# Another order of all pieces of a fused chunk attention and gated convolution, with other homes for the tiles

## The chip, the core and the metric

The kernel runs on one core of a Trainium2 chip. The metric is the time of one execution on the device, in microseconds, as the median of several runs. The core has five engines, each with its own queue that is worked off in order: TensorE (PE, matmuls; PEld is its weight load), VectorE (DVE), ScalarE (ACT), GpSimd (POOL) and SyncE (SP), which here issues every DMA. They wait for one another by semaphores alone.

## The reference

Eight batches, eight heads, 576 positions, 64 numbers a head. Attention is over chunks of 64 positions that don't see each other; its result x, put side by side over the heads (512 channels), goes through a gated convolution.

```python
scores = (1/8) * matmul(q_chunk, k_chunk.T)             # 64 x 64 for each batch, head and chunk
attn = exp(scores - scores.max(-1))
attn = attn / (attn.sum(-1) + 1e-09)
x = matmul(attn, v_chunk)                               # to (batch, 576, 512)
gate = sigmoid(sum over 5 taps of conv_w[k] * x shifted by 4 - k positions, within a batch)
out = ((gate * (x @ w_val)) @ w_out)
```

## The kernel before, in words

The 4608 positions of all batches are cut into 9 groups (g = 0 to 8) of 512. A group is worked in *pieces*: small functions, each of which issues one or a few instructions. The string `ORDER` (line 18 on) lists all 1,131 pieces with their arguments, and the loop at the end of the kernel calls them in that order. Every instruction is issued through one helper (`run`, line 158), which keeps this order on each engine, so all rows of the profile name line 158, and the order of the list is the order of every queue. The table `SLOTS` says which buffer each tile gets, in the order of their creation: `ld` (inputs, 6), `ps` (one PSUM bank each, 4), `big` (two banks each, 2), `acc` (4), `t2` (512 wide, 29, shown as t, t2a to t2r and so on), `t4` (1024 wide, 12). A new tile in a buffer waits until all readers of the old one are through.

The pieces, with g, then the pair p (four of the eight heads, 0 or 1; pair 0 0 is worked in two halves) or the block of 128 channels (0 to 3):

- Loads: `lq`, `lk`, `lv` (q, k, v of a pair, 512 KB), `lw` (128 rows of a weight matrix), `lc` (the taps' table).
- Attention: `S` scores (PE; two of them a pair, 16 instructions each), `mx` their maxima over 64 (DVE). Then one of two ways. Either `sb` subtracts the maxima (DVE), `ex` takes the exponential (ACT), `sm` sums it and takes the reciprocal (DVE, two instructions). Or `ng` scales the maxima (DVE, tiny), `ea` takes exponential and sum in 16 small steps on ACT (32 instructions in the trace), and `rc` finishes the reciprocal (DVE, two tiny ones). `nm` multiplies by the reciprocal (1024 wide). `T` transposes on PE (8 instructions), `ec` copies the result, `A` multiplies by v (PE, 32 instructions).
- x: `xc` copies it from PSUM, `xr` copies it rounded to fp32r, and the remainder x - rounded(x) comes either from `xd` (one subtraction on DVE) or from `xn` and `xe` (PE subtracts with two matmuls against minus the identity, ACT copies).
- Convolution: `k0` the first tap, `k` each of the four others (DVE, a SCALAR_TENSOR_TENSOR on `acc`), `sg` the tanh of it (ACT).
- Value product: `V` (three matmuls of 512 columns: weights and x in high and low part), `F` the same in fp32 for the first group; `vc` copies the result out, `gs` multiplies it with the gate (`gm`: both in one).
- Output product: `gr` rounds, `gd` takes the remainder, `P` three matmuls, `oc` evicts, `st` stores.
- Weights are split into high and low parts in nine small steps (`w1` to `w9`, `wb`); `hl` sets the halo of x; `W` is a number of matmuls without use.

A letter at a name's end puts the piece on another engine: `D` on DVE, `G` on POOL. Without it `nm`, `gd`, `wb` are on POOL, `k0`, `oc`, `xc`, `vc` on ACT, `w1`, `w3`, `w7`, `gs` on DVE. So `gd 0 3` is a remainder on GpSimd and `gdD 0 3` the same on VectorE.

```python
def nm(g, p, *half):
...
    run(on.tensor_tensor, out=out, in0=e, in1=r, op=ALU.mult)
...
def gd(g, m, on=G):
    gl[g, m] = tile_of("gl", [P, T], F32R)
    run(on.tensor_tensor, out=gl[g, m], in0=gt[g, m], in1=gh[g, m].bitcast(F32), op=ALU.subtract)
```

Of the kernel before, what the change touches and what calls it, by code (L numbers as in the profile page):

```python
# [22 lines left out]
F 0 1 0,nm 0 1,lw o 3,F 0 2 0,k0 0 0,w6 v 0,xc 0 0 1,w2 v 3,sb 1 0,w2 v 1,w1G o 0,F 0 3 0,T 0 1,w4 v 3,S 1 1 0,w6 v 2,
lq 2 0,ec 0 1,S 1 1 1,ex 1 0,wb v 2,w4 v 1,wb v 0,A 0 1,lw o 2,lk 2 1,w7 v 3,w5 o 0,W 8,F 0 0 0,w7G v 1,lv 1 0,k0 0 1,
xr 0 1,F 0 2 1,mx 1 1,sm 1 0,w3G o 0,lq 2 1,sb 1 1,k 0 0 4,w1 o 3,S 2 0 0,xc 0 1 0,w2 o 0,nm 1 0,k 0 0 2,ex 1 1,
sm 1 1,xc 0 1 1,w6 v 3,S 2 0 1,xn 0 1,xe 0 1,F 0 3 1,V 0 2 2,hl 1,mx 2 0,T 1 0,sb 2 0,w6 v 1,w3 o 3,w5 o 3,w4 o 0,
F 0 1 1,nm 1 1,k 0 0 1,lq 3 0,S 2 1 0,S 2 1 1,lk 3 0,ec 1 0,lw o 1,ex 2 0,k0 0 3,A 1 0,lv 3 0,F 0 0 1,w5 o 2,mx 2 1,
w7G o 0,xc 1 0 1,wb v 3,sm 2 0,w5 o 1,sb 2 1,w1G o 2,V 0 3 2,lv 1 1,V 0 1 2,k 0 0 3,V 0 0 2,k0G 0 2,w1G o 1,xr 1 0,
w3G o 1,V 0 2 3,w6 o 0,k 0 1 1,T 1 1,xd 1 0,w2 o 2,nm 2 0,xc 1 0 0,ex 2 1,lq 4 0,V 0 0 3,V 0 3 3,ec 1 1,w2 o 3,vc 0 3,
S 3 0 0,wbD v 1,A 1 1,S 3 0 1,k 0 2 4,vc 0 2,k0 1 0,V 1 1 0,V 1 2 0,xr 1 1,sm 2 1,V 1 2 1,mx 3 0,lk 3 1,xd 1 1,  # L30
V 1 1 1,xc 1 1 0,lq 3 1,lv 3 1,ng 3 0,k 0 2 1,V 0 1 3,V 1 2 2,xc 1 1 1,sg 0 0,T 2 0,w3 o 2,lv 2 0,k 0 1 2,V 1 1 2,
gm 0 0,V 1 3 0,k 0 1 4,k 0 3 2,k 0 2 3,nm 2 1,w4 o 3,ea 3 0,k 0 3 1,V 1 2 3,k 0 1 3,k0 1 3,V 1 3 1,V 1 1 3,T 2 1,
# [10 lines left out]
oc 0 0,k0G 2 2,k 2 0 3,P 0 1 3,P 0 3 3,nm 4 0,lq 5 0,oc 0 1,P 0 2 3,k0 2 3,sg 1 1,T 4 0,k 2 1 2,k 2 0 4,V 3 3 0,
xc 3 1 0,k 2 2 2,oc 0 2,V 3 1 0,lk 5 0,rc 4 1,V 3 0 0,gs 1 2,lk 5 1,k 2 3 2,V 3 1 1,ec 4 0,sg 1 3,gs 1 1,S 5 0 0,
sg 2 0,S 5 1 0,k0 3 3,k 2 1 1,S 5 0 1,oc 0 3,S 5 1 1,gs 1 3,mx 5 1,gr 1 0,gd 1 0,nm 4 1,V 3 1 2,gr 1 2,V 3 1 3,
k 2 1 3,V 3 3 1,V 3 2 0,lq 6 0,mx 5 0,V 3 0 1,lk 8 0,k0 3 0,gr 1 1,k 2 2 3,sb 5 0,vc 3 1,sg 2 1,V 3 3 2,ng 5 1,
gdD 1 2,V 3 3 3,lv 4 1,gr 1 3,k 2 2 4,k0 3 2,k 2 3 1,V 3 2 1,gd 1 1,V 3 0 2,lk 6 0,vc 3 3,k 2 3 3,P 1 0 0,ea 5 1,
P 1 1 0,P 1 1 1,k 2 2 1,k 3 2 4,k 3 3 1,lq 6 1,gdD 1 3,P 1 1 2,k 2 3 4,V 3 2 2,k 3 0 2,T 4 1,V 3 0 3,k 3 2 3,k 3 0 1,
V 3 2 3,ec 4 1,P 1 1 3,S 6 0 0,S 6 0 1,A 4 0,lk 6 1,vc 3 2,oc 1 1,sg 2 3,P 1 3 0,gs 2 0,xr 4 0,k 3 0 3,rc 5 1,mx 6 0,
P 1 3 1,P 1 2 0,vc 3 0,P 1 0 1,lv 5 1,xc 4 0 0,xd 4 0,sg 2 2,gs 2 1,ex 5 0,xc 4 0 1,gs 2 3,P 1 2 1,k0 3 1,P 1 0 2,  # L50
P 1 3 2,gr 2 1,V 4 2 0,P 1 2 2,P 1 3 3,lq 7 1,oc 1 3,S 6 1 0,S 6 1 1,gr 2 0,nm 5 1,hl 4,sb 6 0,A 4 1,gd 2 1,k 3 0 4,
gs 2 2,P 1 2 3,V 4 2 1,gr 2 3,k 3 1 2,xr 4 1,P 1 0 3,sm 5 0,sg 3 0,k 3 2 2,gd 2 0,lv 5 0,k0 4 0,nm 5 0,P 2 3 0,xd 4 1,
# [5 lines left out]
xc 5 0 1,gr 3 0,nm 6 0,T 6 0,k 4 2 3,ec 6 0,xd 5 1,k0 5 2,nmD 6 1,k0 5 1,P 2 0 3,oc 2 0,k 4 3 3,V 5 1 1,S 7 0 0,
gd 3 2,S 7 1 0,S 7 1 1,gr 3 1,k0 5 3,S 7 0 1,lk 8 1,k 5 2 2,vc 4 1,lv 6 1,V 4 0 1,k 4 2 2,V 4 0 2,gs 3 3,V 5 0 0,
gr 3 3,k0 5 0,k 4 0 2,mx 7 1,V 4 0 3,V 5 0 1,gd 3 0,st 0 1,mx 7 0,lv 8 1,st 2 1,k 4 0 3,sb 7 1,gdD 3 1,k 4 1 1,gd 3 3,  # L60
V 5 0 2,k 4 2 1,V 5 1 2,vc 4 0,ng 7 0,k 5 2 3,P 3 1 0,k 5 0 3,k 4 0 1,P 3 0 0,P 3 1 1,V 5 1 3,k 4 1 3,V 5 0 3,P 3 1 2,
T 6 1,P 3 0 1,ex 7 1,P 3 1 3,k 4 3 4,k 4 1 2,P 3 0 2,k 4 3 1,k 5 0 4,vc 5 1,ea 7 0,P 3 3 0,lq 8 0,oc 3 1,P 3 3 1,
# [596 lines left out]
```

## Time and profile before

| what | value |
|---|---|
| median of 3 runs | 283.56 us (281.74 to 283.76) |
| profiled execution | 281.89 us, span 280.1 us |
| PE busy | 258.9 us (92%), 3333 matmuls |
| DVE busy | 239.3 us (85%), 330 instructions |
| ACT busy | 195.2 us (70%), 499 instructions |
| POOL busy | 113.1 us (40%), 92 instructions |
| moved by DMA | 42.47 MB, mean 152 GB/s |
| PE's granted clock, mean | 0.994 |

Busy time is what an engine spends in instructions; two that overlap count once. A row of the timeline gives start, length and tiles; neighbours on DVE overlap by some 0.1 us, so the cost of one in a run is the distance of two starts. A wait is put down to the engine whose semaphore came last. Tile names stand without buffer numbers: `big<-ld,ld` are scores, `ps<-t,v_hi` is a value product, `ps<-o_hi,t` an output product, `acc<-x,cw,acc` a tap.

### The profile page before, as it was taken

To read this page: it belongs to the slowest core of one execution; us is meant where nothing else is said; L and a number is where in the kernel's file an instruction comes from. 1 tells how busy PE (TensorE), PEld (TensorE's weight loads), DVE (VectorE), ACT (ScalarE), POOL (GpSimd) and SP (SyncE) were. 2 spreads that over 40 slices of the span, in tenths; PEclk is the share of its full clock that TensorE was granted. 3 is DMA by queue.
4 is the path that set the end of the run, shared out by engine and by line. 5 is a ranking of instruction groups with operands and counts; after the bars stand their busy time and mean duration, and the time that the engine had idled before them with its cause. 6 is when DMAs were issued, how large, how long until landed. Compare 5 with 4: busy or idle time off the path is not lost.

```text
span 280.1 us, 7958 instructions
## 1 busy us (share of the span) xinstructions
PE 258.9 (92%) x3333; PEld 216.6 (77%) x3333; DVE 239.3 (85%) x330; ACT 195.2 (70%) x499; POOL 113.1 (40%) x92
## 2 busy tenths in 40 slices
...
GB/s 230 414 412 411 400 280 53 216 92 288 77 64 239 3 94 210 150 136 170 75 118 0 307 145 192 0 120 220 6 37 0 111 5 152 0 171 16 115 187 150
DMA packets 14291, 42.47 MB, mean 152 GB/s; under 512 B 1712, under 2 KB 1712, under 8 KB 14256
## 3 DMA queue, kind: packets, MB, share of 16 engines
...
HBM read 32.53 MB, written 9.44 MB: 150 GB/s over the span
## 4 chain that ended last, share of the span: by engine, by line
DVE 53%; PE 21%; ACT 14%; DMA 5%; issue 5%; SPq 0%; DVEq 0%; ACTq 0%
DVE acc L158 22%; PE ps L158 19%; DVE t L158 9%; DVE mx L158 5%; DVE rs L158 5%; ACT t L158 5%; DVE e_row L158 4%; ACT e_row L158 4%; DMA acc<-in_moe_w_val 4%; ACT x L158 2%; PE big L158 2%; DMA ld<-in_q 2%; DVE t2q L158 1%; DVE x L158 1%; DVE t4a L158 1%
## 5 line engine op out<-in xcount | busy, mean ns | idle before, releaser
L158 DVE SCALAR_TENSOR_TENSOR acc<-x,cw,acc 128x516 f32<-128x516 f32 (+1 forms) x144 | 111.7, 817 | 3.2 <-ACT acc L158 2.9
L158 PE MATMUL ps<-t,v_hi 128*128 128x512 f32 x240 | 85.1, 395 | 2.9 <-ACT t2f L158 2.1
L158 PEld LDWEIGHTS ps<-t,v_hi 128*128 128x128 f32 x240 | 45.5, 190 | 11.5 <-ACT t2f L158 2.5
L158 PE MATMUL ps<-t,v_lo 128*128 128x512 f32 x120 | 45.9, 383 | 0.0
L158 POOL TENSOR_TENSOR t<-e_row,rs 128x1024 f32<-128x1024 f32 (+1 forms) x12 | 23.2, 1936 | 30.0 <-DVE rs L158 30.0
L158 PEld LDWEIGHTS big<-ld,ld 64*64 64x64 f32 x1152 | 19.5, 139 | 15.0 <-issue 9.7
L158 ACT ACTIVATE e_row<-big,mx 128x64 f32<-128x64 f32 x96 | 28.6, 357 | 2.5 <-DVE mx L158 2.5
L158 PE MATMUL big<-ld,ld 64*64 64x64 f32 x1152 | 22.0, 226 | 8.7 <-DMA ld<-in_q 6.6
L158 PE MATMUL ps<-o_hi,t 128*128 128x512 f32 x80 | 29.9, 381 | 0.0
L158 ACT COPY x<-big 128x512 f32<-128x512 f32 (+3 forms) x42 | 19.7, 520 | 12.5 <-PE big L158 6.2
L158 DVE TENSOR_REDUCE mx<-big 128x16 f32<-128x1024 f32 (+1 forms) x19 | 21.8, 1151 | 5.1 <-PE big L158 5.1
L158 PEld LDWEIGHTS ps<-t,v_lo 128*128 128x128 f32 x120 | 22.8, 190 | 3.3 <-issue 0.5
L158 ACT ACTIVATION_READ_ACCUMULATOR e_row<-big,mx 128x1 f32 x96 | 23.8, 249 | 0.0
L158 PE MATMUL big<-t,ld 64*64 64x64 f32 x1088 | 19.4, 220 | 4.4 <-issue 2.4
L158 PEld LDWEIGHTS big<-t,ld 64*64 64x64 f32 x1088 | 17.6, 135 | 6.7 <-issue 2.1
L158 ACT COPY t<-ps 128x512 f32<-128x512 f32 x27 | 16.7, 625 | 8.4 <-PE ps L158 5.8
L158 ACT ACTIVATE t<-big 128x1024 f32<-128x1024 f32 x15 | 15.8, 1077 | 7.1 <-PE big L158 7.1
L158 ACT ACTIVATE e_row<-e_row 128x1024 f32<-128x1024 f32 (+1 forms) x12 | 12.0, 1001 | 11.4 <-DVE e_row L158 11.4
L158 ACT CAST t<-big 128x1024 fp32r<-128x1024 f32 x17 | 17.3, 1019 | 2.0 <-PE big L158 2.0
L158 ACT ACTIVATE acc<-x,cw 128x516 f32<-128x516 f32 (+1 forms) x24 | 17.8, 756 | 0.0
L158 POOL TENSOR_SCALAR acc<-x,cw 128x516 f32<-128x516 f32 (+1 forms) x9 | 14.9, 1657 | 4.8 <-ACT x L158 4.8
L158 PEld LDWEIGHTS ps<-o_hi,t 128*128 128x128 f32 x80 | 15.1, 189 | 2.2
...
## 6 DMA issues: line engine op xcount, KB each, us to landing
...
```

The lines of the kernel that those rows point to most:

```text
L158: return tc.keep_in_program_order(fn(*args, **kwargs))
```

## The change

All pieces are listed in another order and `SLOTS` gives other buffers; no function changes. By the two lists (1,131 pieces before, 1,134 after) the following changes besides the order:

- `ea` 6 to 7: pairs 5 0, 6 1, 7 1, 8 1 take the place of 4 1, 5 1, 7 0 (3 0, 4 0 and 8 0 stay); `sb`, `sm`, `ex` one less each, `ng` and `rc` one more.
- `xn`/`xe` 2 to 4 (1 0, 1 1, 2 0, 3 1 instead of 0 1, 2 1); `xd` 15 to 13.
- `nm` on DVE 3 to 7 (one of them a half), on POOL 16 to 12. `gd` on DVE 11 to 16, on POOL 25 to 20. `oc` on DVE 8 to 11, on ACT 28 to 25. `xc` on DVE 4 to 5 pieces.
- `k0` on ACT 24 to 19, on POOL 9 to 13, on DVE 3 to 4.
- `wb` on DVE 4 to 1, on POOL 4 to 7; `w1` on DVE 4 to 2, on POOL 5 to 7; `w3` on DVE 4 to 6, on POOL 5 to 3. `gm` 2 to 1, `vc` and `gs` one more each.

```diff
-ORDER = """zi,lk 0 0,zw,zr 1,lc,lq 0 0,lw v 2,lk 0 1,w1 c 0,S 0 0 1,w3G c 0,lq 0 1,lw v 0,mx 0 0 1,sb 0 0 1,S 0 0 0,lw v 3,
+ORDER = """lk 0 0,lq 0 0,zr 1,S 0 0 0,mx 0 0 0,lq 0 1,lc,sb 0 0 0,zw,lk 0 1,S 0 0 1,w3 c 0,w1 c 0,lw v 2,mx 0 0 1,lw v 0,
...
 SLOTS = dict(
-    ld="012345012350412305241203123142135013450420534024035425",
+    ld="012345012340512304152403240104120354251041045342502402",
...
```

**The first DMAs, on SP.** Before; `ld` tiles are q, k and v, `acc` tiles are raw weights, `raw_cw` is the taps' table:

```order
L158 DMA ld_75<-in_k 128x1024
L158 DMA raw_cw<-in_moe_conv_w 128x40
L158 DMA ld_81<-in_q 128x1024
L158 DMA acc_83<-in_moe_w_val 128x1024
L158 DMA ld_85<-in_k 128x1024
L158 DMA ld_108<-in_q 128x1024
L158 DMA acc_110<-in_moe_w_val 128x1024
L158 DMA acc_132<-in_moe_w_val 128x1024
L158 DMA ld_134<-in_k 128x1024
```

After:

```order
L159 DMA ld_71<-in_k 128x1024
L159 DMA ld_73<-in_q 128x1024
L159 DMA ld_95<-in_q 128x1024
L159 DMA raw_cw<-in_moe_conv_w 128x40
L159 DMA ld_101<-in_k 128x1024
L159 DMA acc_124<-in_moe_w_val 128x1024
L159 DMA acc_127<-in_moe_w_val 128x1024
L159 DMA acc_147<-in_moe_w_val 128x1024
L159 DMA ld_176<-in_v 128x1024
```

The taps' table went from second to fourth, q from third to second; the second half's q and k stand ahead of all weights, and three parts of `w_val` follow before k of the next pair.

**DVE, about pair 8 1.** Before, from the reciprocal of its sums (`rs_2680`) to its normalisation (`t4a<-e_row_65,rs_2680`):

```order
L158 RECIPROCAL rs_2680<-rs_2680 128x16
L158 SCALAR_TENSOR_TENSOR t2s<-t_2630,t2d 128x512
L158 SCALAR_TENSOR_TENSOR acc_2265<-x_2129,cw,acc_2265 128x516 x2
L158 SCALAR_TENSOR_TENSOR acc_2269<-x_2129,cw,acc_2269 128x516
L158 TENSOR_SCALAR t_2703<-big_2661 128x1024
L158 SCALAR_TENSOR_TENSOR t_2708<-t2i,t2m 128x512
L158 SCALAR_TENSOR_TENSOR t2q<-t2e,t_2050 128x512
L158 SCALAR_TENSOR_TENSOR t2g<-t2a,t_2354 128x512
L158 TENSOR_SCALAR acc_2794<-x_2621,cw 128x516
L158 SCALAR_TENSOR_TENSOR acc_2794<-x_2621,cw,acc_2794 128x516
L158 TENSOR_REDUCE mx_2816<-big_2715 128x16
L158 TENSOR_TENSOR t4a<-e_row_65,rs_2680 128x1024
```

After, from the reciprocal of its sums (`rs_2816`, summed by ScalarE) to its normalisation (`t_3065`):

```order
L159 TENSOR_SCALAR rs_2816<-rs_2816 128x16
L159 RECIPROCAL rs_2816<-rs_2816 128x16
L159 TENSOR_REDUCE mx_2954<-big_2917 128x16
L159 TENSOR_TENSOR t_2956<-t2c,t2n 128x512
L159 TENSOR_SCALAR mx_2954<-mx_2954 128x16
L159 SCALAR_TENSOR_TENSOR acc_2765<-x_2594,cw,acc_2765 128x516
L159 TENSOR_SCALAR acc_3018<-x_2861,cw 128x516
L159 SCALAR_TENSOR_TENSOR acc_2761<-x_2594,cw,acc_2761 128x516
L159 SCALAR_TENSOR_TENSOR acc_2765<-x_2594,cw,acc_2765 128x516
L159 TENSOR_TENSOR t2h<-t2m,t_2867 128x512
L159 SCALAR_TENSOR_TENSOR acc_2761<-x_2594,cw,acc_2761 128x516
L159 TENSOR_TENSOR t_3065<-e_row_65,rs_2816 128x1024
```

The reduction that stood ahead of the reciprocal (`TENSOR_REDUCE rs`) is gone, two small instructions are in its place, and two remainders of y (`t_2956<-t2c,t2n` and `t2h<-t2m,t_2867`, both `gdD`) stand between, where before there were products with the gate.

**PE, at the first value products of the last group.** `t_3331` is its rounded x, `t_3357` the remainder that DVE's `xd 8 0` writes. Before:

```order
L158 MATMUL ps_3187<-o_hi,t_3141 128x512
L158 MATMUL ps_3187<-o_lo,t_3141 128x512
L158 MATMUL ps_3187<-o_hi,t_3155 128x512
L158 MATMUL ps_3368<-t_3331,v_hi 128x512
L158 MATMUL ps_3368<-t_3331,v_lo 128x512
L158 MATMUL ps_3368<-t_3357,v_hi 128x512
L158 MATMUL ps_3376<-t_3331,v_hi 128x512
L158 MATMUL ps_3376<-t_3331,v_lo 128x512
L158 MATMUL ps_3376<-t_3357,v_hi 128x512
L158 MATMUL ps_3345<-o_hi,t2m 128x512
L158 MATMUL ps_3345<-o_lo,t2m 128x512
L158 MATMUL ps_3345<-o_hi,t2p 128x512
```

After (`t_3341` and `t_3350`):

```order
L159 MATMUL ps_3355<-o_hi,t_2867 128x512
L159 MATMUL ps_3355<-o_lo,t_2867 128x512
L159 MATMUL ps_3355<-o_hi,t2h 128x512
L159 MATMUL ps_3396<-t_3341,v_hi 128x512
L159 MATMUL ps_3396<-t_3341,v_lo 128x512
L159 MATMUL ps_3396<-t_3350,v_hi 128x512
L159 MATMUL ps_3405<-t_3341,v_hi 128x512
L159 MATMUL ps_3405<-t_3341,v_lo 128x512
L159 MATMUL ps_3405<-t_3350,v_hi 128x512
L159 MATMUL ps_3396<-t_3341,v_hi 128x512
L159 MATMUL ps_3396<-t_3341,v_lo 128x512
L159 MATMUL ps_3396<-t_3350,v_hi 128x512
```

The value products of the last group follow output products in both; after the first of them stand 195 matmuls to the end, where there were 201, and 30 matmuls lie between the place of `xd 8 0` in the list and the first of them, where there were 6.

## Rows read from the trace of the kernel before

**Rows 1.** The page, part 1: busy us of each engine (share), instructions.
```profile
PE 258.9 (92%) x3333; PEld 216.6 (77%) x3333; DVE 239.3 (85%) x330; ACT 195.2 (70%) x499; POOL 113.1 (40%) x92
```

**Rows 2.** Chain of waits, 228 to 280: start us, length us, what.
```profile
231.91 1.22 DVE t L158
...
233.18 43.24 PE ps L158 x199
...
276.44 0.59 ACT t L158
```

**Rows 3.** Waits of DVE: waited for, us in total, times, longest.
```profile
DVE mx L158 <- PE big L158: 5.1, 3, 3.3
DVE t L158 <- ACT x L158: 3.4, 2, 2.0
```

**Rows 4.** Timeline of DVE, 160 to 187: start us, us, instruction, [idle before].
```profile
160.95 10.74 DVE L158 SCALAR_TENSOR_TENSOR acc<-x,cw,acc 128x516 f32<-128x516 f32 x16
...
177.61 1.23 DVE L158 TENSOR_TENSOR t<-big,t 128x1024 fp32r<-128x1024 f32 x1 [1.97 <-ACT x L158]
178.75 1.23 DVE L158 TENSOR_REDUCE rs<-e_row 128x16 f32<-128x1040 f32 x1
...
180.18 0.63 DVE L158 SCALAR_TENSOR_TENSOR t2s<-t,t2d 128x512 f32<-128x512 f32 x1
...
185.18 0.68 DVE L158 SCALAR_TENSOR_TENSOR t2g<-t2a,t 128x512 f32<-128x512 f32 x1
185.78 0.48 DVE L158 TENSOR_SCALAR acc<-x,cw 128x516 f32<-128x516 f32 x1
186.18 0.75 DVE L158 SCALAR_TENSOR_TENSOR acc<-x,cw,acc 128x516 f32<-128x516 f32 x1
```

**Rows 5.** Timeline of PE, 131 to 139.
```profile
131.18 1.91 PE L158 MATMUL big<-ident,t 128*128 128x128 f32 x16
132.85 0.46 PE L158 MATMUL ps<-o_hi,t2r 128*128 128x512 f32 x1
...
136.26 2.10 PE L158 MATMUL big<-t,ld 64*64 64x64 f32 x128
138.29 0.48 PE L158 MATMUL ps<-o_hi,t2q 128*128 128x512 f32 x1
```

**Rows 6.** Timeline, DVE beside POOL, four places.
```profile
21.99 1.08 DVE L158 SCALAR_TENSOR_TENSOR t<-t,t 128x512 uint32<-128x512 uint32 x1
...
40.87 1.58 POOL L158 TENSOR_SCALAR acc<-x,cw 128x512 f32<-128x512 f32 x1
...
41.36 1.41 DVE L158 SCALAR_TENSOR_TENSOR acc<-x,cw,acc 128x512 f32<-128x512 f32 x2
...
147.43 1.34 POOL L158 TENSOR_TENSOR t2s<-t,t2l 128x512 fp32r<-128x512 f32 x1 [3.83 <-ACT t2l L158]
...
147.56 1.77 DVE L158 SCALAR_TENSOR_TENSOR acc<-x,cw,acc 128x516 f32<-128x516 f32 x1
...
255.68 1.18 DVE L158 SCALAR_TENSOR_TENSOR t2c<-t2l,t 128x512 f32<-128x512 f32 x1
```

**Rows 7.** Timeline of SP, the first issues.
```profile
1.15 0.42 SPq L158 DMA_DIRECT2D raw_cw<-in_moe_conv_w  x1
1.62 0.42 SPq L158 DMA_DIRECT2D ld<-in_q  x1
```

**Rows 8.** By stretch: busy us of PE, PEld, DVE, ACT, POOL; PEclk granted; DMA.
```profile
70.00:80.00 10.00, 10.00 (x55) 8.67 (x55) 9.97 (x16) 9.21 (x40) 2.17 (x1) 1.00 0.14 54
140.00:150.00 10.00, 7.93 (x34) 6.50 (x33) 8.83 (x10) 4.86 (x10) 4.75 (x3) 0.85 0.22 83
```

**Rows 9.** Timeline of PE and DVE, 145 to 153.
```profile
145.80 0.48 PE L158 MATMUL ps<-t,v_hi 128*128 128x512 f32 x1 [2.06 <-ACT t2f L158]
...
152.27 1.42 DVE L158 SCALAR_TENSOR_TENSOR acc<-x,cw,acc 128x516 f32<-128x516 f32 x2 [2.93 <-ACT acc L158]
```

**Rows 10.** Chain of waits, 73 to 80.
```profile
73.84 4.85 ACT e_row L158 x32
```

**Rows 11.** Groups by line: busy us, mean ns, idle before.
```profile
L158 PE MATMUL big<-t,minus 128*128 128x512 f32 x4 | 1.4, 423 | 0.0
```

More of the change, by code (lines that the diff above doesn't have):

```diff
@@ L23 @@
[L23 to L32, printed above, removed]
@@ L43 @@
[L43 to L52, printed above, removed]
@@ L58 @@
[L58 to L62, printed above, removed]
@@ new lines @@
+hl 3,oc 0 1,gr 1 2,mx 5 0,V 3 1 1,lq 5 1,k 2 0 4,ng 5 0,k 2 2 4,xc 3 1 1,V 3 0 0,V 3 2 0,xr 3 1,xc 3 1 0,k 2 3 4,
+k 2 2 2,lq 6 0,k 2 1 2,nm 4 0,k0 3 0,lq 7 0,V 3 2 1,lk 5 1,k 2 0 2,k 2 1 4,k 3 0 3,xn 3 1,xe 3 1,ea 5 0,lk 6 0,
+k 2 0 1,V 3 3 0,V 3 3 1,k 2 1 3,V 3 3 2,k 3 0 2,gd 1 1,T 4 0,k 2 1 1,k 2 3 1,ec 4 0,V 3 3 3,k 2 2 1,V 3 2 2,V 3 2 3,
+V 3 0 1,sg 2 0,gd 1 0,k 3 0 4,vc 3 3,gs 2 0,V 3 1 2,S 5 1 0,k 2 2 3,S 5 1 1,k 2 3 3,ex 4 1,gdD 1 2,k 3 0 1,gr 1 3,
+vc 3 2,rc 5 0,A 4 0,sg 2 2,P 1 3 0,gdD 1 3,nm 5 0,V 3 0 2,sm 4 1,V 3 0 3,xc 4 0 1,k0 3 1,V 3 1 3,gr 2 0,mx 5 1,
@@ new lines @@
+k0 6 2,V 6 1 2,k0 6 0,xr 7 0,gs 4 1,k 6 0 4,gs 5 3,V 5 1 2,ea 8 1,V 6 0 2,st 3 0,gs 4 3,V 5 1 3,V 6 2 0,k 6 3 4,
+k 6 2 3,xd 7 0,V 6 2 1,k 6 0 3,vc 5 1,V 6 2 2,gr 4 2,xc 7 0 0,V 6 3 0,gr 5 3,V 6 0 3,T 7 1,k 6 2 1,vc 6 0,gdD 4 0,
+V 6 2 3,V 6 3 1,gr 4 3,k 6 1 4,xcD 7 0 1,gs 5 2,gr 4 1,hl 7,V 6 1 3,V 6 3 2,sg 5 0,V 6 3 3,ec 7 1,S 8 0 0,S 8 0 1,
+gd 4 2,rc 8 1,mx 8 0,gdD 4 1,vc 6 1,ng 8 0,vc 6 3,A 7 1,P 4 3 0,P 4 0 0,vc 6 2,P 4 1 0,P 4 2 0,k 6 0 2,P 4 3 1,
+k0D 7 1,P 4 1 1,sg 5 1,P 4 2 1,k 6 3 1,st 3 3,gd 4 3,st 1 2,k0G 7 0,P 4 1 2,k 6 1 2,ea 8 0,gdD 5 3,k 6 3 3,P 4 0 1,
```

132 lines of the change are left out of this document (74 added, 58 removed).

## The prediction

> **What bounds the kernel now.** I read the page first. TensorE (PE) is busy 258.9 us of 280.1 and VectorE (DVE) 239.3 [rows 1]: both are near full, ScalarE (ACT) and GpSimd (POOL) are not, so which of the two limits a stretch has to be read from who hands over to whom. The chain of waits shows the end: the last remainder of x (`xd 8 0`) ends on DVE at 233.13, and from 233.18 PE works through 43.24 us without a gap, then one eviction and a store, until 280.1 [rows 2]. So the time is DVE's clock at the last remainder, plus PE's work behind it, plus a tail of 3.7 us. Ahead of that, DVE is what PE waits for; it idles itself for 5.1 us on scores (3.3 of them at the start) and 3.4 on ScalarE [rows 3], little beside its work. A TensorE that is 92% busy is the wrong place to look for what an order changes: its work is fixed, and what it loses is what DVE hands over late.
>
> Hence the measure: at a handover, DVE's work ahead of it in the order plus PE's work behind it. Waits come on top in both kernels.
>
> **Unit prices**, by starts in a run of work [rows 4]: a tap (`k`) 10.74 / 16 = 0.67 us; a full-width operation (`mx`, `sb`, `xd`, `nm`) 1.14; `sm` with its reciprocal 1.43; a 512-wide one (`gs`, `gd`, `w4`, `w7`, `wb`, `oc`) 0.60; `k0` 0.40. PE takes 43.24 / 199 = 0.217 a matmul [rows 2], 0.84 for eight transposes (1.67 for two times eight) and 2.03 for the 64 instructions (128 records) of two products [rows 5].
>
> **The price of GpSimd.** A tap that starts 0.13 us behind a `gd` on POOL takes 1.77 us instead of 0.67 [rows 6]: it waits until POOL's instruction is over. POOL's one-input `k0` beside two taps costs them nothing: 1.41 us for both [rows 6]. In the timeline 22 two-input DVE operations stand over 0.2 us above their price, the first at 21.99, the last at 255.68 [rows 6], 16.9 us together; 19 of them, 14.2 us, before 233. POOL has 42 two-input operations there (`nm`, `gd`, `wb`, `w7`), so I charge DVE 0.34 us for each, between 0 and 1.1 by the single rows.
> The Trainium skill, page "SBUF — State Buffer", section "Who interferes with whom", says that a DVE instruction with two SBUF inputs and a GpSimd instruction that reads SBUF exclude each other for a whole instruction. For `gd` the trace agrees (1.77); for the one-input `k0` it does not (1.41 for two); by the page this change, which gives POOL four more `k0`, would be worth less (a rival below).
>
> **The change, part by part.** Counted from the two lists up to `xd 8 0` (DVE):
> - Pair 5 0, 6 1, 7 1, 8 1 instead of 4 1, 5 1, 7 0 on ScalarE sums: one `sb` (1.14) and one `sm` (1.43) less, `ng` and `rc` more (0.4 with all): -2.1.
> - Two remainders to TensorE: two `xd` less, -2.3. PE gets four matmuls more, 0.42 us each alone [rows 11], 0.217 in a run: +0.9. They stand in groups 1 to 3, where ScalarE's `xr` and `xe` (no row for the wait; between 0 and 1 us each) are in PE's way.
> - Normalisation from POOL to DVE: three and a half `nm` more, +4.0. Four `gd` more, +2.4; two `gs` more and a `gm` less, +0.6; `k0` and `xc` +0.9; `oc` -0.6.
> - Weights: three `wb` less, two `w1` less, two `w3` more (one the taps' small one): -2.0. Two taps less ahead: -1.3.
> Sum -0.4 us. Then POOL has 36 two-input operations ahead instead of 42: 6 x 0.34 = -2.0. So DVE reaches `xd 8 0` 2.4 us earlier if its waits stay.
> - PE's work behind: 195 matmuls from `V 8 2 0` instead of 201: -1.3.
> At this handover the sum is **-3.7 us**.
>
> It must not be that another handover is the tighter one. Before, the tightest that I find is `gdD 3 1` to `P 3 1 1`: ahead 72 taps (48.0), 34 full-width operations (38.6), 9 `sm` with 15 reciprocals (13.6), 37 of 0.60 (22.3), the half-size first pair and small ones (10.7), together 133.2; 33 x 0.34 = 11.2; behind 468 matmuls, 40 transposes and 256 instructions of products, 113.1 (with 0.2155 a matmul): 257.5. The same at `V 8 2 0`: 198.1 + 14.2 + 43.3 = 255.6. In the changed order the tightest is `sb 6 0`, which lets `T 5 1` go: 53 taps, 27 full-width, 8 `sm`, 29 of 0.60 and small ones, 104.1; 23 x 0.34 = 7.8; behind 579 matmuls, 64 transposes, 416 instructions of products, 144.5: 256.4; at `V 8 2 0` it is 197.7 + 12.2 + 42.0 = 251.9. By the tightest the change gains **1.1 us**, by the last **3.7**. Before, PE still waits at 145.8 and 233.2 [rows 2, 9], behind the tight place as well as at it, so I take the middle, **-2.4**.
> - Start: q goes out second instead of third. Its issue starts at 1.62, that of the taps' table ahead of it at 1.15 [rows 7]: -0.5, between 0 (if the landing is what counts) and -0.5. The key and query of the second half and three parts of w_val follow sooner, one later: nothing, since DVE has work then.
> - ScalarE: 4.85 us for one pair's sums [rows 10] less one `ex`, two copies (`xe`) more, five `k0` and three `oc` less: about +1 of 195 busy. It is covered by a ScalarE that is 70% busy; without that cover it is rival 3.
> - The end (evict, store) is the same: 0.
>
> Sum: -2.4 - 0.5 = **-2.9 us**, from 281.89 of the profiled execution to 279.0. That execution lies 1.7 under the median of the three runs; against the median, 283.56 - 2.9 = **280.7 us**. Ends of the unknown prices: -3.7 - 0.5 at one side, +1 (four matmuls and their waits, no gain) at the other: 279.4 to 284.6.
>
> **Rivals.**
> 1. *The port turns against it: slower.* DVE now does more operations with two SBUF inputs (7 `nm`, 16 `gd`, 35 `gs` in all, where it had 3, 11, 34), and each that starts behind a `nm` or `gd` of POOL waits up to 1.1 us [rows 6]. Place: taps and `gd` of groups 2 to 6. Forecast is 36 x 0.34 = 12.2 us; at 0.56 a piece it is 20.2, 8 more: 288.7. The point is where it eats 5.7 us beyond the forecast (286.4): 0.50 a piece. For: a row like 1.77 is no rarity, and the order decides the neighbours. Against: fewer POOL operations. 0.14.
> 2. *No gain: the one-input operations of POOL exclude too.* Then all of POOL's reads count: two-input ones 6 less, one-input ones (`k0`, `w1`, `w3`) four more, net 2 less instead of 6, so 4 x 0.34 = 1.4 us is lost, and with the tight place of 1.1 alone it is 283.56 - 1.1 - 0.5 + 1.4 = 283.4. This is the page's rule above. Also where the waits simply grow by what the balance gives. 0.22.
> 3. *ScalarE's block.* A pair's sums hold ScalarE 4.85 us [rows 10]; `gr`, `vc` and `xr` behind them wait. If PE stands for half of one block that was not there: +2.4 on the forecast, 283.1, two blocks 285.5. Against: before, PE is busy all of 70 to 80 [rows 8], where such a block stands. 0.06.
> 4. *The half clock goes: faster.* At 145.80 PE comes out of a wait of 2.06 us [rows 9]; in 140 to 150 its granted clock is 0.85 on the mean, with a share at the lower of its two levels (1.2 and 2.4 GHz) [rows 8], and DVE then stands 2.93 us [rows 9]. If the other order has no such hole: 280.7 - 2.9 = 277.8. For: by the same sums DVE's list ahead of group 5's first matmuls (`xd 5 0`) is 8.4 us longer than PE's now, 11.6 before. Against: any wait of this length may bring it back elsewhere. 0.18.
> The forecast has 0.40, about half of it on each side of 280.7.
>
> **How the numbers follow.** The likeliest case is the forecast, 280.7. The range reaches from rival 4 with the last handover as the only tight one (277.8 - 1.3 = 276.5) to the point of rival 1: 276.5 to 286.5; what lies outside is most of rival 1 and the far end of rival 4. About 1% is what a measurement of this kernel can tell from no change. Faster by over 1% (below 280.7): half of the forecast, rival 4 and a little of 2: 0.42. Within: the other half, rivals 2 and 3: 0.39. Slower (above 286.4): rival 1 and the far end of 3: 0.19.
>
> **What would show it.** In the profile after: the last unbroken PE run should start near 230 and have about 195 matmuls; DVE's busy time stay within 2 us of 239; POOL's fall by some 4; the two-input rows above their price sum to 14 or so, not over 20. If DVE waits longer for PE or ScalarE than in the rows here, the balance was not the limit, and I am wrong by that. If a `k0` of POOL is seen to hold a tap, rival 2 is at work; a granted clock of 0.99 or more in every slice of the middle would show rival 4.

## The result, and the profile after

The changed kernel takes 274.11 us (median of 4 runs, 273.17 to 274.39) beside 283.66 of the kernel before: ratio 0.967, 95% interval 0.962 to 0.972. Run again in the last experiment it took 273.97, ratio 0.967 (0.964 to 0.971). The forecast was 280.7 in a range from 276.5. It missed by 6.6 us and lies outside the range, on the fast side. The profiled execution took 273.97 us, its span 272.2.

The page's part 1, answering [rows 1], and the granted clock in 40 slices:

```profile
PE 257.4 (95%) x3337; PEld 217.2 (80%) x3337; DVE 241.3 (89%) x338; ACT 196.0 (72%) x525; POOL 108.4 (40%) x90
...
PEclk9999999999999999999999999999999999999999
```

The engines do about the same work as before (VectorE 2.0 us more, GpSimd 4.7 less), in 8 us less. So it is mostly idle time that went, not work. The chain of waits from 140 on (start us, length us, what), answering [rows 2]:

```profile
148.18 2.17 DVE acc L159
150.35 1.14 DVE t L159
151.49 0.14 issue
151.63 1.06 PE big L159 x8
152.69 4.54 PE ps L159 x21
...
207.77 2.02 PE big L159 x128
209.79 58.52 PE ps L159 x270
```

The last handover from VectorE to TensorE is no longer `xd 8 0` at 233 but `xd 5 0` (150.35), which lets `T 6 0` start at 151.63. From there to 268.3 TensorE works for 117 us without a wait. `xd 8 0` itself now starts at 222.46, where it started at 231.91 [rows 2]:

```profile
222.46 1.21 DVE L159 TENSOR_TENSOR t<-big,t 128x1024 fp32r<-128x1024 f32 x1
```

VectorE's waits, answering [rows 3] (waited for, us in total, times, longest), and one stretch, answering [rows 8]:

```profile
DVE mx L159 <- PE big L159: 9.4, 7, 6.7
...
DVE t L159 <- ACT t L159: 0.3, 1, 0.3
```

```profile
140.00:150.00 10.00, 10.00 (x201) 8.46 (x190) 9.82 (x12) 6.58 (x16) 8.29 (x6) 1.00 0.63 213
```

Of the 9.4 us of waiting for scores 6.7 are the start. The rows `t <- ACT x` (3.4 us) and the 2.93 us for `acc` are gone. TensorE has no gap between 140 and 150, and its granted clock there is 1.00 instead of 0.85.

### The profile page after: what moved, and what is told of

It reads as the page before. It is cut to its first block, busy times and chain, and to the rows that moved or that the text cites. A ratio compares the mean times of both kernels' runs of the same rounds, so it can differ in the third digit from the quotient of the medians.

```text
span 272.2 us, 7986 instructions
## 1 busy us (share of the span) xinstructions
PE 257.4 (95%) x3337; PEld 217.2 (80%) x3337; DVE 241.3 (89%) x338; ACT 196.0 (72%) x525; POOL 108.4 (40%) x90
## 4 chain that ended last, share of the span: by engine, by line
PE 70%; DVE 25%; issue 2%; DMA 2%; POOL 0%; ACT 0%; SPq 0%; DVEq 0%; POOLq 0%
PE ps L159 55%; PE big L159 14%; DVE acc L159 11%; DVE t L159 4%; DVE mx L159 3%; DMA ld<-in_q 2%; DVE rs L159 1%; DVE t2m L159 1%; DVE e_row L159 1%; DVE t2f L159 1%; DVE t2e L159 1%; DVE t2a L159 0%; POOL t L159 0%; DVE t2l L159 0%; DVE t2j L159 0%
## 5 line engine op out<-in xcount | busy, mean ns | idle before, releaser
L159 PE MATMUL ps<-t,v_hi 128*128 128x512 f32 x232 | 80.1, 388 | 0.0
L159 PE MATMUL ps<-o_hi,t 128*128 128x512 f32 x104 | 38.4, 386 | 0.0
L159 ACT ACTIVATE e_row<-big,mx 128x64 f32<-128x64 f32 x112 | 33.3, 358 | 1.5 <-DVE mx L159 1.5
L159 POOL TENSOR_SCALAR acc<-x,cw 128x516 f32<-128x516 f32 (+1 forms) x13 | 24.8, 1905 | 12.3 <-ACT x L159 11.0
L159 PE MATMUL ps<-o_lo,t 128*128 128x512 f32 x72 | 27.3, 379 | 0.0
L159 PEld LDWEIGHTS ps<-o_hi,t 128*128 128x128 f32 x104 | 19.6, 189 | 2.8
L159 ACT COPY t<-ps 128x512 f32<-128x512 f32 x15 | 8.9, 600 | 16.6 <-PE ps L159 16.5
L159 PEld LDWEIGHTS big<-ident,t 128*128 128x128 f32 x128 | 14.7, 141 | 4.6 <-issue 2.5
L159 PE MATMUL big<-ident,t 128*128 128x128 f32 x128 | 16.7, 274 | 1.5 <-DVE t L159 1.5
L159 POOL COPY x<-x 128x16 f32<-128x16 f32 x8 | 4.4, 547 | 34.6 <-DVE acc L159 34.6
```

The source lines that it names most:

```text
L159: return tc.keep_in_program_order(fn(*args, **kwargs))
```

## The experiments

All ratios are against the kernel before, run on the same chip in the same session; where a difference between two runs is given "by the medians", it is the plain difference of their times. "List" is the string `ORDER`.

### Waits for a copy that stands ahead: three runs

In the trace before, two remainders on VectorE, and the copy that stands ahead of a third, start at the very moment at which a *copy* of x on ScalarE ends, though the rounding that the remainder needs was done earlier. The rows of VectorE for the first two (the third is the row at 177.61 in [rows 4]), then ScalarE's around 143 for the opposite case:

```profile
65.10 1.23 DVE L158 TENSOR_TENSOR t<-big,t 128x1024 fp32r<-128x1024 f32 x1 [1.47 <-ACT x L158]
...
85.03 0.75 DVE L158 COPY x<-big 128x384 f32<-128x384 f32 x2 [1.41 <-ACT x L158]
```

```profile
143.15 0.59 ACT L158 COPY x<-big 128x512 f32<-128x512 f32 x1 [2.44 <-DVE t L158]
143.63 0.72 ACT L158 ACTIVATE t2n<-acc 128x192 f32<-128x192 f32 x2
144.26 1.00 ACT L158 CAST t<-big 128x1024 fp32r<-128x1024 f32 x1
145.15 0.60 ACT L158 COPY t2f<-ps 128x512 f32<-128x512 f32 x1
```

Both only read the PSUM tile `big`. In the built program `xd 2 0` waits for ScalarE's copy `xc 2 0 0`, and `xc 5 0 0` for VectorE's `xd 5 0`: two readers of one PSUM tile on two engines follow each other as listed. The Trainium skill, page "PSUM — Partial Sum Buffer", section "PSUM bank collisions raise a hardware error", says that the compiler's scheduler puts such a dependency between any two instructions on different engines that touch the same bank in the same 32 partitions, reads included; the rows agree. At 143 the wait costs TensorE as well: the eviction `t2f` stands behind the waiting copy, and TensorE waits 2.06 us for it [rows 9].

First run: five copies are listed behind the remainder of their tile.

```diff
-xc 2 0 1,
 V 1 3 3,sg 0 1,W 1,vc 1 3,
-xc 2 0 0,
 xd 2 0,
...
 ex 3 1,
+xc 2 0 1,xc 2 0 0,
...
-xc 3 0 1,
...
 xcD 3 0 0,xd 3 0,gs 0 3,w6 o 2,
+xc 3 0 1,
...
-xc 6 1 0,
...
-xc 6 1 1,
 xd 6 1,
+xc 6 1 0,xc 6 1 1,
```

> The kernel before, with five copies of x (xc) on ScalarE listed behind the remainder (xd) of the same PSUM tile instead of ahead of it, for the pairs 2 0, 3 0 and 6 1; VectorE's order is unchanged, no engine gets another operation. Theory A (the gain of the change came from waits: a remainder on VectorE waits for every copy on ScalarE that is listed ahead of it on the same PSUM tile, 1.47 + 1.41 + 1.97 us in the trace before): these three waits shrink to about 0.5 us together, VectorE reaches xd 8 0 about 4 us earlier, and the time falls by 3 to 4.4 us, to 279.3 to 280.7. Rival B (the gain came from the balance of the engines, waits of VectorE are made good elsewhere): within 1 us of the kernel before, 282.7 to 284.7, with other waits of the same sum in VectorE's list.

Measured: 281.16 us against 282.95, ratio 0.990 (0.986 to 0.994), that is 1.6 to 3.8 us. VectorE at the first and the third place:

```profile
65.17 1.21 DVE L158 TENSOR_TENSOR t<-big,t 128x1024 fp32r<-128x1024 f32 x1
...
176.04 1.21 DVE L158 TENSOR_TENSOR t<-big,t 128x1024 fp32r<-128x1024 f32 x1
```

No wait stands behind them in brackets; of 4.85 us at the three places 0.9 is left. The ten executions scatter from 278.6 to 284.1 us, more than the gain. The time falls by somewhat less than expected; the interval of the ratio leaves out B's "within 1 us".

Second run: one copy changes places with one remainder.

```diff
-xd 5 0,xc 5 0 0,
+xc 5 0 0,xd 5 0,
```

> The kernel before, with one copy on ScalarE (xc 5 0 0) listed ahead of the remainder xd 5 0 instead of behind it; no engine's own order changes, only who waits for whom. In the trace before the copy stands 2.45 us until the remainder ends at 143.1, and an eviction behind it keeps TensorE waiting 2.06 us until 145.8, after which 3.4 us run at the lower clock. Theory A (waits): the wait of 2.06 and the stretch at the lower clock go, and with ScalarE earlier the 2.93 us for which VectorE stands at 152.27 shrink; the time falls by 1.5 to 4 us, to 279.7 to 282.2. Rival B (TensorE only waits later, for the last remainder on VectorE at 232): within 0.7 us of the kernel before.

Measured: 280.13, ratio 0.991 (0.988 to 0.994), 1.7 to 3.4 us less. TensorE has no wait from 142 to 150, and VectorE's 2.93 us at 152 are 0.33. This comes out as A says. The stretch at the lower clock can come back elsewhere, though: the profiled execution (281.77, the slowest of the eight) has it behind a wait of 1.34 us at 70.56.

```profile
152.12 1.42 DVE L158 SCALAR_TENSOR_TENSOR acc<-x,cw,acc 128x516 f32<-128x516 f32 x2 [0.33 <-ACT acc L158]
```

```profile
70.00:80.00 10.00, 9.44 (x54) 8.07 (x54) 9.97 (x15) 7.11 (x25) 2.85 (x2) 0.83 0.38 118
140.00:150.00 10.00, 10.00 (x168) 8.88 (x168) 9.90 (x16) 8.01 (x16) 6.93 (x6) 1.00 0.48 135
```

Third run: both edits.

> The two edits before together (six copies moved in the list, nothing else). Theory A: the gains add up, 5 to 8 us, to 275.7 to 278.7, most of what the change brought. Rival B: no more than 1 us. If only the first edit counts since VectorE sets the end: as a1.

Measured: 277.03, ratio 0.980 (0.973 to 0.986), 5.8 us less by the ratio. The two gains add up. VectorE's idle time ahead of `xd 8 0`, summed over its timeline, falls from 19.7 to 14.5 us, and the last stretch starts 4.6 us earlier:

```profile
227.27 1.22 DVE t L158
228.54 43.24 PE ps L158 x199
```

Six list entries, with no engine's work and no buffer changed, give three fifths of what the whole change gives.

### The wait put back

The changed kernel, with two copies ahead of a remainder:

```diff
+xc 5 1 1,xc 5 1 0,
 xd 5 1,S 7 0 0,gs 3 2,
-xc 5 1 1,xc 5 1 0,
```

> The changed kernel with two copies of x on ScalarE (xc 5 1 1, xc 5 1 0) listed ahead of the remainder xd 5 1 instead of behind it; no engine's order changes. The copies end at 140.0 in the trace of the changed kernel, the remainder starts at 137.4. Theory A (such a wait is worth what it delays VectorE by, as long as TensorE waits for VectorE later): a new wait of 2.6 us at the remainder, the handover sb 7 0 to A 5 0 (0.13 us of slack) and xd 5 0 to T 6 0 (0.15) come as much later: 2 to 2.6 us slower, 276.1 to 276.7. Rival B (TensorE bounds the changed kernel, VectorE has room): under 0.7 us.

Measured: 276.94, ratio 0.979 (0.973 to 0.985), 2.8 us more than the changed kernel by the medians. VectorE, then TensorE at the next handover, then the stretch behind it:

```profile
139.70 1.22 DVE L159 TENSOR_TENSOR t<-big,t 128x1024 fp32r<-128x1024 f32 x1 [2.65 <-ACT x L159]
```

```profile
148.21 1.98 PE L159 MATMUL big<-t,ld 64*64 64x64 f32 x64 [3.47 <-issue]
```

```profile
150.00:160.00 10.00, 10.00 (x49) 8.45 (x43) 8.65 (x12) 8.29 (x20) 5.33 (x4) 0.81 0.31 106
```

The wait appears with the size that was read from the trace, the handover comes later, and behind the hole of 3.47 us the clock is at its lower level for a part of the stretch (0.81 on the mean). So two misplaced copies make all three marks of the kernel before again.

### The engines exchanged

80 pieces that stand on different engines in the two kernels (nm, gd, oc, k0, xc, ec, w1, w3, w7, wb) get the engine of the other kernel; the lists stay.

```diff
-nm 2 1
+nmD 2 1
-xcD 3 0 0
+xc 3 0 0
...
```

> The kernel before in its own order, with all 80 operations that stand on another engine in the changed kernel moved there (normalisation, remainders of the gate, evictions, seeds of the taps, weights). Theory A (the order and its waits made the gain): VectorE gets 4.8 us more work ahead of xd 8 0 by the unit prices, GpSimd fewer two-input operations (worth up to 2): slower by 1 to 5 us, 284.7 to 288.7. Rival B (the homes made it): faster by most of the 9.5 us, 274 to 278.

Measured: 296.14 in the median of four executions, 291.61 to 298.35, beside 282.95. There is no interval; even the fastest is 8.7 us slower, more than A expected, and B is out. In the profiled execution (296.16) `xd 8 0` starts at 244.6, 12.7 us later. 4.8 us are the added work by the unit prices, and the two-input operations above their unit price sum to 25.7 us (each start to the next start, less the price from [rows 4]; good to about half a microsecond, by which small operations are counted), where they sum to 19.2 before. A tap on VectorE, and GpSimd beside it:

```profile
112.59 2.07 DVE L158 SCALAR_TENSOR_TENSOR acc<-x,cw,acc 128x516 f32<-128x516 f32 x1
```

```profile
112.21 1.90 POOL L158 TENSOR_TENSOR t<-e_row,rs 128x1024 f32<-128x1024 f32 x1
```

> The changed kernel in its own order, with the same 80 operations back on the engines that they have in the kernel before. By unit prices VectorE has 5.3 us less ahead of xd 8 0 than in the changed kernel. Theory A1 (the order alone carries the gain): 274.1 or up to 5 us faster, 269 to 275. Theory A2 (an order fits one set of homes: moved operations meet GpSimd's two-input ones on the shared port, as when the kernel before took the homes of the changed one and became some 13 us slower, 6.5 of them taps above their price): slower than the changed kernel by 3 to 13 us, 277 to 287, with the sum of two-input operations above their price over 20 us instead of 17.

Measured: 291.30, ratio 1.030 (1.024 to 1.035): 17 us slower than the changed kernel, though VectorE has 5.3 us less to do ahead of `xd 8 0`. The sum above price is 28.5 instead of 17.1, and VectorE's idle time ahead of `xd 8 0` 22.8 instead of 12.8. A2 is right, and more strongly than it said: an order fits one set of engines. Neither the engines in the old order nor the order with the old engines is good alone, so the two have no separate price.

### Parts of the change undone

```diff
-xn 1 0,xe 1 0,
+xd 1 0,
...
-xn 3 1,xe 3 1,
+xd 3 1,
```

> The changed kernel with the remainders of x of the pairs 1 0 and 3 1 on VectorE again (xd) instead of by TensorE (xn, xe); everything else stays. VectorE gets 2.3 us more before 100, TensorE four matmuls less (0.9), ScalarE two copies less. Theory A (the sum at a handover): xd 5 0 and T 6 0 come 2.3 us later, so 1.5 to 2.3 us slower, 275.6 to 276.4. Rival B (the copies xe and their waits cost as much as they save): within 0.7 us, or faster.

Measured: 276.53, ratio 0.978 (0.973 to 0.983), 2.4 us more than the changed kernel by the medians; `xd 8 0` comes 2.5 us later, and so does `T 6 0`, at 154.09 instead of 151.63. A holds; the time lies just above its range.

```profile
154.09 1.06 PE L159 MATMUL big<-ident,t 128*128 128x128 f32 x8 [1.46 <-DVE t L159]
```

```diff
-ng 6 1
+sb 6 1
...
-ea 6 1
+ex 6 1
...
-rc 6 1
+sm 6 1
```

> The changed kernel with the exponentials of the pair 6 1 summed on VectorE (sb, one ex, sm) instead of ScalarE (ng, ea, rc): six such pairs instead of seven. VectorE gets 2.1 us more at 133 to 142, ScalarE loses 3.6. Theory A (the sum at a handover): xd 5 0 and T 6 0 come 2 us later, 1.5 to 2.1 us slower, 275.6 to 276.2. Rival B (ScalarE's block is what holds): the same or up to 1.5 us faster, since gr and xc behind the block go sooner.

Measured: 274.06, ratio 0.971 (0.965 to 0.976): not told apart from the changed kernel. Three executions take 273.9 to 274.3 us and one 276.05, so the interval alone does not rule out A. Its mechanism is not there, however: `T 6 0` does not come 2 us later (151.69 for 151.63).

```profile
151.69 1.06 PE L159 MATMUL big<-ident,t 128*128 128x128 f32 x8 [0.47 <-DVE t L159]
```

VectorE's busy time is 241.7 instead of 241.3, since 1.6 us less stands above price (15.5 instead of 17.1): other neighbours at the port paid for the added work. The seventh pair brought nothing that can be measured.

### The start and the rest

What is left between the run with six copies moved and the changed kernel, 3.6 us by the ratios (2.9 by the medians), was looked for at the start.

```diff
-lc,lq 0 0,lw v 2,lk 0 1,
+lq 0 0,lw v 2,lk 0 1,lc,
```

> The kernel before with the six copies moved as in the run of both edits (277.0 us, ratio 0.980), and the DMA of the taps' table (lc) issued behind the first query and key (lq 0 0, lk 0 1) instead of ahead of them. Theory (the start term of the forecast): the first scores start 0.5 us earlier, so 0.3 to 0.5 us less than with the copies alone, 276.5 to 276.7; up to 1.1 if the landing moves by more than the issue, as between the two profiles (6.57 and 5.46). Rival: 0 (277.0), the landing sets it and the queue does not.

Measured: 278.44, ratio 0.982 (0.979 to 0.986): no gain. VectorE's row says why:

```profile
9.45 0.18 DVE L158 TENSOR_SCALAR cw_t<-raw_cw 128x20 f32<-128x20 f32 x1 [8.34 <-DMA raw_cw<-in_moe_conv_w]
```

The table of 20 KB lands behind the large loads, and the maxima are queued behind the instruction that waits for it. In the next run the table goes one place later only.

```diff
-lc,lq 0 0,lw v 2,
+lq 0 0,lc,lw v 2,
```

> The kernel before with the six copies moved (277.0 us) and the taps' table issued directly behind the first query, one place later than before, where the run with it behind the second key let VectorE wait until 9.45 for it. Theory: the query's issue is 0.47 us earlier and VectorE's wait for the table stays under the wait for the scores: 0.3 to 1.0 us less, 276.0 to 276.7. Rival: the same 277.0 within 0.4, since the landing of the query is set by the 512 KB of the key ahead of it.

Measured: 277.62, ratio 0.977 (0.974 to 0.981). The interval overlaps that of the copies alone: not told apart. In its profile the first scores start at 5.74, where they start at 7.71 with the copies alone, but VectorE waits again at 12.5 and 17.6; its idle time ahead of 30 us is 9.7 us, with the copies alone 8.8. The other direction, the queue of before in the changed kernel:

```diff
-lk 0 0,lq 0 0,...,lq 0 1,lc,...,lk 0 1,...,lw v 2,
+lk 0 0,lc,lq 0 0,lw v 2,lk 0 1,...,lq 0 1,
```

> The changed kernel with only SyncE's first six issues in the order of the kernel before (table of the taps second, query third, w_val ahead of the second key and query). Theory (the start is a part of what the six moved copies left open, some 3 us): the first scores start 0.5 to 1.1 us later and the second half of them later still, behind 512 KB of w_val; nothing later gives it back, since VectorE has under 0.8 us of idle time at any one place from 22 to 240: 0.5 to 2 us slower, 274.6 to 276.1. Rival (the start is hidden by work that VectorE finds anyway): within 0.4 of 274.1.

Measured: 275.78, ratio 0.971 (0.968 to 0.974), 1.2 us more by the ratio; the intervals just overlap. In the profile TensorE's first row stands at 7.50 and VectorE's `xd 8 0` at 224.96, 2.5 us later than in the changed kernel:

```profile
7.50 1.77 PE L159 MATMUL big<-ld,ld 64*64 64x64 f32 x56 [7.50 <-DMA ld<-in_q]
```

So the start may be worth some 1 to 2 us there; in the old order the two runs found nothing. To build the rest up from the old order, the remainders of 1 0 and 3 1 went to TensorE, on top of the run with the table behind the second key; the copies of these pairs are listed ahead.

```diff
-xd 1 0,
...
+xn 1 0,
 ec 1 1,
+xe 1 0,
...
-xd 3 1,
...
+xn 3 1,
 P 0 0 2,P 0 0 3,oc 0 0,
+xe 3 1,
```

> The run before it, with the remainders of x of the pairs 1 0 and 3 1 also formed by TensorE (xn, xe) instead of VectorE (xd), as in the changed kernel. Theory (the gain of the change is the sum of removed waits, of the start and of work taken from VectorE ahead of its last handover): 2.3 us less on VectorE, as putting them back into the changed kernel cost 2.4: 274.2 to 275.2, that is most of the way to the 274.1 of the changed kernel. Rival (what is left of the gain needs the whole other order): 276 or more.

Measured: 278.91, ratio 0.985 (0.981 to 0.988): no gain, the rival. The sum above price rose from 17.3 to 19.3 us, which is nearly all of the 2.3 us that VectorE was relieved of. The remaining 3 to 4 us could not be rebuilt from parts in the old order; that stays open, and no run tells the order from the buffers in it. The traces of the run with six copies moved and of the changed kernel only say where it lies: of the 4.8 us by which `xd 8 0` comes earlier (227.27 and 222.46), 3.1 are VectorE's work ahead of it, the port included, and 1.7 its idle time.

### Order at the port

The changed kernel's last wait of TensorE is for `xd 5 0`, which stands behind a tap of 2.24 us. VectorE and GpSimd there:

```profile
148.10 2.24 DVE L159 SCALAR_TENSOR_TENSOR acc<-x,cw,acc 128x516 f32<-128x516 f32 x1
150.27 1.21 DVE L159 TENSOR_TENSOR t<-big,t 128x1024 fp32r<-128x1024 f32 x1
```

```profile
147.89 1.90 POOL L159 TENSOR_TENSOR t<-e_row,rs 128x1024 f32<-128x1024 f32 x1
149.76 1.72 POOL L159 TENSOR_TENSOR t<-t2a,t 128x512 fp32r<-128x512 f32 x1
```

The tap has two SBUF inputs and stands until GpSimd is through; the remainder, one of whose inputs is in PSUM, takes its 1.21 us beside the next one. First try: `xd 5 0` ahead of the tap, and the table of the taps behind `lk 0 1`.

```diff
-lc,lk 0 1,
+lk 0 1,lc,
...
-xcD 5 0 0,k 4 0 3,
+xcD 5 0 0,xd 5 0,k 4 0 3,
...
-xd 5 0,
```

> The changed kernel with the remainder xd 5 0 on VectorE ahead of the tap k 4 0 3 and the copy xc 5 0 1, and the taps' table (lc) issued behind lk 0 1. In the trace of the changed kernel TensorE waits 1.68 us at 150 for this remainder, the last wait before a stretch of 117 us without one. Theory A (the last handover sets the end): T 6 0 starts 1.3 us earlier; the next places have 0.4 to 0.8 us of room (S 8 0 0, T 8 0), so 0.4 to 1.0 us less, 273.1 to 273.7. Rival B (VectorE's sum binds at the next handover too): 274.1 within 0.4.

Measured: 275.77, ratio 0.972 (0.969 to 0.976): 1.5 us slower than the changed kernel. With the pair 4 0 by TensorE as well:

```diff
-xd 4 0,
+xn 4 0,xe 4 0,
```

> The run before it, with the remainder of the pair 4 0 by TensorE too (xn 4 0, xe 4 0 in place of xd 4 0). VectorE has 1.14 us less from 112 on, TensorE two matmuls more (0.43 to 0.86) and ScalarE a copy of 1 us. Theory A (VectorE's sum ahead of the handovers after 112 sets the end): 1.0 to 2.0 us less than the changed kernel, 272.1 to 273.1. Rival B (TensorE's own work sets it, 95 percent busy): 0 to 0.9 us more than the run before it. Rival C (ScalarE, 1 us later with gr 2 2 and ec 4 1 behind it, holds TensorE): 274 or more.

Measured: 276.07, ratio 0.974 (0.971 to 0.977). Two things went wrong in both. The table was late again (VectorE waits 0.32 and 1.20 us for it, and its idle time ahead of 30 us is 9.9 and 10.1 us, in the changed kernel 8.3 and, run again, 8.8), and at `xd 5 0` nothing was won, since the next tap met the next operation of GpSimd (the two taps take 2.80 us, in the changed kernel 2.24 and 0.74):

```profile
150.45 1.21 DVE L159 TENSOR_TENSOR t<-big,t 128x1024 fp32r<-128x1024 f32 x1
151.59 2.80 DVE L159 SCALAR_TENSOR_TENSOR acc<-x,cw,acc 128x516 f32<-128x516 f32 x2
```

In the second run VectorE also waits 1.81 us for the scores `S 6 0`, where it waits 0.89 us in the first: rival C, as the row has it. By the time alone, 0.3 us more than the first run, rival B fits as well.

Second try: the queue as it was, and two reads of PSUM in a row ahead of the taps.

```diff
-xcD 5 0 0,k 4 0 3,k0G 5 2,xc 5 0 1,...,xd 5 0,k 4 2 4,nm 6 1,mx 7 1,
+xcD 5 0 0,xd 5 0,mx 7 1,k 4 0 3,k0G 5 2,xc 5 0 1,...,k 4 2 4,nm 6 1,
```

> The changed kernel with xd 5 0 and mx 7 1 on VectorE ahead of the taps k 4 0 3 and k 4 2 4 (the queue of DMAs stays). Both read PSUM and stand beside two-input operations of GpSimd (nm 6 1, gd 3 3), beside which a tap took 2.24 us. Theory A (the last wait of TensorE, 1.68 us at 150, sets the end): T 6 0 starts 1.3 us earlier, 0.4 to 1.0 us less, 273.1 to 273.7. Rival B (VectorE's sum binds at the next handover, and the tap meets the next operation of GpSimd): 274.1 within 0.4. That the run with the earlier remainder lost 1.4 us would then lie in the DMA of the taps' table alone.

Measured: 272.92, ratio 0.961 (0.958 to 0.964). VectorE:

```profile
147.74 1.21 DVE L159 TENSOR_TENSOR t<-big,t 128x1024 fp32r<-128x1024 f32 x1
148.87 1.21 DVE L159 TENSOR_REDUCE mx<-big 128x16 f32<-128x1024 f32 x1
150.00 3.00 DVE L159 SCALAR_TENSOR_TENSOR acc<-x,cw,acc 128x516 f32<-128x516 f32 x3
```

Three taps in 3.00 us, and TensorE's transposes start at 149.69 instead of 151.63. The first try had one read ahead and the later table, this one two reads and the old queue; no run tells apart which of the two differences decides. The same exchange at three more places:

```diff
+mx 4 0,
 k 1 2 4,
...
-mx 4 0,
...
+xc 4 1 0,xr 4 1,xd 4 1,
 k 3 1 1,
...
-xc 4 1 0,xr 4 1,
...
-xd 4 1,
...
+gs 3 2,
 xd 5 1,S 7 0 0,
-gs 3 2,
```

> The run with xd 5 0 and mx 7 1 early (272.9 us, ratio 0.961), and at three more places a VectorE operation that GpSimd does not hold changes places with one that it does: mx 4 0 ahead of the tap k 1 2 4 (1.70 us beside gd 0 2), xd 4 1 ahead of the tap k 3 1 1 (1.69 beside gd 2 2; the copy and the rounding that it needs are listed ahead too), gs 3 2 ahead of xd 5 1 (gs 1.66 beside nm 6 0). Each engine does the same work. Theory (a two-input operation on VectorE that starts behind a two-input one on GpSimd waits for it; one that reads PSUM does not): about 1 us each leaves the sum above price, 16.5 to 13.5 or 14; VectorE is that much earlier at the handovers behind them, and the time falls by 1 to 2.5 us, to 270.4 to 271.9. Rival (the exclusion only finds the next two-input operation, as when xd 5 0 alone went ahead of the tap; or TensorE's own work is all that is left): within 0.5 of 272.9.

> The changed kernel itself, on the same chip as the run beside it, for a ratio that can be set against it: 274.1 us, 0.967 of the kernel before.

Measured: 270.78, ratio 0.957 (0.952 to 0.961), beside 273.97 and 0.967 (0.964 to 0.971) of the changed kernel on the same chip. The intervals stand apart: about 3 us faster than the changed kernel, the fastest version here. Its page, and the second of the places (in the changed kernel a `gs` takes 1.76 us there):

```profile
PE 258.0 (95%) x3337; PEld 217.5 (80%) x3337; DVE 238.5 (88%) x338; ACT 195.7 (72%) x525; POOL 107.4 (40%) x90
```

```profile
119.50 1.22 DVE L159 TENSOR_TENSOR t<-big,t 128x1024 fp32r<-128x1024 f32 x1
120.64 0.75 DVE L159 SCALAR_TENSOR_TENSOR acc<-x,cw,acc 128x516 f32<-128x516 f32 x1
121.30 0.68 DVE L159 SCALAR_TENSOR_TENSOR t2m<-t,t2i 128x512 f32<-128x512 f32 x1
```

```profile
119.32 1.76 DVE L159 SCALAR_TENSOR_TENSOR t2m<-t,t2i 128x512 f32<-128x512 f32 x1
```

(The last fence is the changed kernel.) VectorE is busy 2.8 us less with the same operations, and the sum above price is 14.2 us instead of 17.2. At the third place the wait mostly moves on: `gs 3 2` is free, but the next `gs` takes 1.47 us, where it took 0.68. This profiled execution was the slowest of the six (273.22), with 2.1 us more idle time of VectorE ahead of `xd 8 0` than in the changed kernel, so its chain doesn't show the gain of the median; the busy time does.

## Why the prediction was wrong, step by step

**The step that failed is "Waits come on top in both kernels".** The measure took VectorE's waits as equal before and after. The starts of `xd 8 0` split into its two terms: VectorE's work ahead of it is 212.2 us before (231.91 less 19.74 idle) and 209.7 after (222.46 less 12.79). That is 2.5 us less; the forecast said 2.4. The idle time is 7.0 us less; the forecast said 0, but for 0.5 at the start. The rows were there: [rows 3] lists 3.4 us of `t <- ACT x`, which the prediction called little beside its work, and [rows 9] the 2.93 and 2.06, which only rival 4 took up. Of VectorE's 19.7 us of idle time ahead of `xd 8 0` the prediction named 8.5 in its account of the bound. The work it summed right (198.1 + 14.2 = 212.3 before, 197.7 + 12.2 = 209.9 after); the waits it read as a background, and did not ask of each what it waits for. Five waits of the trace before, at 65, 85, 145, 152 and 178, are gone, 8.3 us together, and 1.3 us more stand at other places. Three of the five are waits for a copy, and the other two follow from ScalarE's own wait at 143: in the run with that one copy moved 0.33 us of them is left. So it is the order of two readers of one tile, which is a property of the list, and the change rewrites the list. It does not simply put the remainders first: six of its 13 still have a ScalarE copy listed between the rounding and the remainder (five of 15 before), but ScalarE is through with it in time. The runs with the moved copies show these waits to be worth 5.8 us (3.9 to 7.6), and the run that puts one back 2.8.

**The place of the last handover.** Forecast: an unbroken run from near 230, about 195 matmuls. Found: from 151.63 on, with 270 matmuls of 512 columns in its last piece alone. With VectorE 9.4 us earlier at `xd 8 0`, TensorE doesn't wait there. The place that sets the end was not `sb 6 0` either, the tightest by the sums, but `xd 5 0`: a mean charge for the port could not say that the tap just ahead of it would be one that stands for 2.24 us.

**Port.** Forecast: six two-input operations of GpSimd fewer, 2.0 us less above price. Found: 2.1 less (19.2 to 17.1, over the whole run); by the prediction's own count, rows more than 0.2 above price, 16.9 before and 13.8 after, where it said 14 or so. The number is right by luck, the reasoning behind it is not: exchanging the engines moved this sum by +6.5 and +11.4 us, relieving VectorE of two remainders by +2.0, and four exchanges in the list by -3.0. It counts neighbours, not operations. Rival 1 had this mechanism and its price; the change lay on the good side of it.

**Start.** Forecast -0.5; the first scores start 1.1 us earlier in the two profiles (5.46 for 6.57; in the four runs on the old queue that were profiled later it is 7.5 to 7.8). What that is worth depends on what waits behind it: nothing in the old order, perhaps 1 to 2 us in the changed one. VectorE's idle time ahead of 30 us is about the same in both profiles, 8.2 and 8.3 us.

**The parts.** Two remainders by TensorE: forecast 2.3 less on VectorE, 2.5 when undone in the changed kernel, nothing in the old order. The seventh pair: forecast 2.1 less, no later handover when undone.

**Rival 4, the half clock goes,** is what happened, at 0.18 and with 277.8. It was priced as one stretch of lower clock beside an unchanged rest. The hole came from the same cause as VectorE's waits, so it went together with them; removing that hole alone gave 2.5 us. The clock itself is the smaller part: of the 57 executions of the kernel before beside the later runs, the 18 with a mean granted clock of 0.997 or more take 282.4 us on the mean and the 37 with 0.992 to 0.994 take 283.7. Rival 2 shows only in a fraction (last section), and rival 3 not: with one block of ScalarE less the time is not lower.
